# Output projection cut at the last attention head, with its first part placed before that head is finished

## The chip, the cores and the metric

The kernel runs on one core of a Trainium2 chip. The metric is the device time of one execution, in microseconds (us). Before the change it was 695.34 us in three runs (692.23 to 695.98). The span of a trace is a little shorter than the device time: a trace of 688.7 us belongs to a run of 690.84 us.

## The reference

One decoding step of a transformer block: a modulation from a condition vector, attention of one query over a cache of 16,384 positions in 32 heads, output projection, layer norm, and a gated feed-forward block.

```python
h = layernorm(x) * (1 + ca) + sa
q = (h @ wq)                                   # 32 heads of 128
p = softmax(q . k_cache * 128**-0.5)           # 16384 positions per head
o = p . v_cache                                # [32, 128]
x = x + ga * (o.reshape(1, 4096) @ wo)         # output projection, 4096 -> 640
h = layernorm(x) * (1 + cb) + sb
x = x + gb * ((silu(h @ w_gate) * (h @ w_up)) @ w_down)   # 640 -> 1728 -> 640
```

Keys and values are 268 MB of the 290 MB that are read.

## The kernel before

The program keeps a list of instructions for each engine, in the order in which they are added; semaphores order them across engines. `op_P1` sums a key block's products to scores on TensorE, `op_BC` spreads the maximum of the scores over the partitions, `op_EXP` (ScalarE) takes the exponential and the row-sums, `op_PV` multiplies the probabilities with the values ("P.V": 32 matmuls of 512 columns), `op_EV` (ScalarE) copies the result out of PSUM, and `op_OT` turns it into one column per head with four small matmuls.

```python
for h in range(H + 1):
    if h >= 1:
        op_PV(h - 1, 0); op_PV(h - 1, 1)
    if h < H:
        op_P1(h, 0)
    if h >= 1:
        op_OT(h - 1)
    if h < H:
        op_P1(h, 1); op_BC(h)
    # ... V1, V2, V3, NB on VectorE, EV, A3, DG, EXP on ScalarE ...

lsum_ps = pb[0]
pl = prog.add("pe", lambda e: e.matmul(lsum_ps[:, 0:H], lhsT=ones_f, rhs=rowsum[:, 0:H], ...), ...)
d = prog.add("dve", lambda e: e.reciprocal(rinv_all[:, :], lsum_ps[:, 0:H]), ...)
d = prog.add("dve", lambda e: e.tensor_tensor(otn[:, :], otf[:, :], rinv_all[:, :], ALU.mult), ...)

def pe_wo(e):                                   # 160 matmuls of one column
    for j in range(KC):                         # KC = 5 blocks of 128 outputs
        for h in range(H):
            ins = e.matmul(attn_ps[:, j:j + 1], lhsT=wo_v[:, h, j * P:(j + 1) * P],
                           rhs=otn[:, h:h + 1], start=(h == 0), stop=(h == H - 1))
# ... layer norm; 140 gate and up matmuls; silu; 70 down matmuls in four pieces,
#     each waiting for the landing of its piece of the weights; output ...
```

So the projection waits for all 32 heads: the normalisation of the last one stands ahead of all 160 matmuls.

## Time and profile before

| | before |
|---|---|
| span of the trace | 692.0 us |
| transfers: share of the span in which the 16 engines are busy | 98.6%, 420 GB/s |
| last P.V | 661.70 to 670.46 us |
| output projection ends | 677.65 us, 7.19 after the last P.V |
| down projection starts; last down weights land | 687.31; about 685 us |

The page of before shows, in this order, the span, the busy time of each engine with its share and its instructions, the queue of the data transfers (packets, MB, share), and the chain that ended last by engine.

```profile
span 692.0 us, 5506 instructions
...
PE 509.0 (74%) x2434; PEld 210.1 (30%) x2435; DVE 493.0 (71%) x289; ACT 60.8 (9%) x178; POOL 1.5 (0%) x10
...
q1 hardware_dynamic: 18078, 290.48, 98.6%
...
DMA 45%; DVE 28%; PE 23%; ACT 2%; issue 1%; SPq 0%
...
```

The transfers fill the span: 98.6% busy, at 420 GB/s. At that rate the kernel can get much faster only by moving fewer bytes; what remains is how long the tail lasts after the last keys are there. The timeline of before shows that tail. Columns: start in us, duration, engine, line of the kernel, operation, output and inputs, shapes, count; in brackets the idle time of the engine before it and what ended it. "PE" is TensorE's matmuls, "PEld" its weight loads; "issue" is idle time that no recorded dependence explains.

```profile
...
660.30 0.49 PE L533 MATMUL psum_all<-diag,ones_f 128*128 128x128 f32 x2 [1.54 <-ACT diag L527]
...
661.70 8.76 PE L557 MATMUL psum_all<-arena,p_bf 128*4 128x512 bf16 x32 [0.91 <-ACT p_bf L545]
...
670.49 0.59 ACT L565 ACTIVATE ot_sb<-psum_all 4x512 f32<-4x512 f32 x1 [8.84 <-PE psum_all L557]
...
671.13 1.05 PE L574 MATMUL psum_all<-ident_f,ot_sb 4*128 4x1 f32 x8 [0.68 <-ACT ot_sb L565]
...
672.11 0.41 PE L610 MATMUL psum_all<-rowsum,ones_f 128*128 128x32 f32 x2
...
672.55 0.36 DVE L613 RECIPROCAL rinv_all<-psum_all 128x32 f32<-128x32 f32 x1 [11.43 <-PE psum_all L610]
672.94 0.19 DVE L615 TENSOR_TENSOR otn<-otf,rinv_all 128x32 bf16<-128x32 f32 x1
...
673.24 4.41 PE L630 MATMUL psum_all<-otn,arena 128*128 128x1 bf16 x160 [0.72 <-issue]
...
681.45 4.40 PE L672 MATMUL psum_all<-h_bf,arena 128*128 128x1 bf16 x140 [1.14 <-DVE psum_all L663]
...
687.31 2.09 PE L699 MATMUL psum_all<-a_bf,arena 128*128 128x1 bf16 x70 [1.46 <-issue]
...
```

Read it as a chain. The last P.V (L557) ends at 661.70 + 8.76 = 670.46. TensorE then waits 0.68 us for ScalarE's copy (L565), does the transposes (L574) and the row-sum of all heads (L610), and waits 0.72 us, marked "issue", which is really the reciprocal and the multiplication on VectorE (L613, L615). Then come the 160 projection matmuls (L630). The two holes are what the change aims at. TensorE also waits 0.91 us just before the last P.V: a place to put something.

The window view of before, over the last P.V in two parts; the third number from the end is the granted TensorE clock:

```profile
...
661.70:666.00 4.30, 4.30 (x13) 1.39 (x14) 0.00 (x0) 0.00 (x0) 0.00 (x0) 0.60 1.06 377
666.00:670.40 4.40, 4.40 (x21) 1.59 (x19) 0.00 (x0) 0.00 (x0) 0.00 (x0) 1.00 1.03 411
...
```

The first half of the last P.V ran at a mean granted clock of 0.60, the second at 1.00.

### The profile page before, as it was taken

The page shows a single profiled execution, that of the slowest core. Times are in us where ns is not written, and L with a number is a line of the kernel's source. Part 1 is how long each engine was busy: PE and PEld are TensorE (multiplying, and loading weights), DVE is VectorE, ACT ScalarE, POOL GpSimd, SP SyncE. Part 2 cuts the span into 40 slices and gives each one's busy share as a digit, 9 for nine tenths or more (in the row PEclk, how much of TensorE's full clock was granted, in tenths as well). Part 3 has the DMA queues.
Part 4 walks back from the last instruction along what each step waited for, and adds up shares of the span by engine and source line. Part 5 has one row for each costly group of instructions (what it writes and reads, how often), then busy time and mean ns, then how long its engine had stood idle before and what let it go on. Part 6 is the DMA issues. An engine that isn't in the chain of part 4 may idle for free.

```text
span 692.0 us, 5506 instructions
## 1 busy us (share of the span) xinstructions
PE 509.0 (74%) x2434; PEld 210.1 (30%) x2435; DVE 493.0 (71%) x289; ACT 60.8 (9%) x178; POOL 1.5 (0%) x10
## 2 busy tenths in 40 slices
PE   1458868678778768688888685778688677687876
PEld 1222323233332323233333232323223223233335
DVE  1077777778887777778886777778877777778811
ACT  1020100000000000000000000000000000000000
POOL 0000000000000000000000000000000000000000
PEclk9976969878888969688879698877969879888785
DMA  8999999999999999999999999999999999999994
GB/s 345 432 443 425 424 431 444 426 425 428 441 430 427 428 439 429 430 428 435 434 429 428 435 432 430 429 430 435 430 434 427 432 433 434 428 423 437 390 392 158
DMA packets 18101, 290.82 MB, mean 420 GB/s; under 512 B 1244, under 2 KB 7070, under 8 KB 8990
## 3 DMA queue, kind: packets, MB, share of 16 engines
q1 hardware_dynamic: 18078, 290.48, 98.6%
q8 instruction: 19, 0.31, 0.2%
q14 instruction: 4, 0.03, 0.0%
HBM read 290.47 MB, written 0.00 MB: 420 GB/s over the span
## 4 chain that ended last, share of the span: by engine, by line
DMA 45%; DVE 28%; PE 23%; ACT 2%; issue 1%; SPq 0%
DMA arena<-in_A_k_cache_dram 45%; DVE arena L488 16%; PE psum_all L557 14%; DVE arena L494 9%; PE psum_all L506 6%; DVE s_sb L515 1%; PE psum_all L533 1%; ACT diag L527 1%; ACT p_bf L545 1%; PE psum_all L630 1%; PE psum_all L672 1%; DVE m L522 1%; DVE nbias L539 1%; SPq L727 0%; PE psum_all L699 0%
## 5 line engine op out<-in xcount | busy, mean ns | idle before, releaser
L488 DVE TENSOR_TENSOR arena<-arena,qbc 128x8192 bf16<-128x8192 bf16 x64 | 282.9, 4420 | 42.0 <-DMA arena<-in_A_k_cache_dram 41.9
L557 PE MATMUL psum_all<-arena,p_bf 128*4 128x512 bf16 x1024 | 280.5, 443 | 29.1 <-ACT p_bf L545 29.1
L506 PE MATMUL psum_all<-arena,ident_bf 128*128 128x512 bf16 x512 | 151.0, 448 | 72.3 <-DVE arena L494 72.2
L557 PEld LDWEIGHTS psum_all<-arena,p_bf 128*4 128x4 bf16 x1024 | 95.2, 95 | 205.4 <-issue 78.8
L494 DVE TENSOR_TENSOR arena<-arena 128x4096 bf16<-128x4096 bf16 x64 | 146.7, 2292 | 2.2
L506 PEld LDWEIGHTS psum_all<-arena,ident_bf 128*128 128x128 bf16 x512 | 50.8, 109 | 151.8 <-DVE arena L494 79.0
L515 DVE TENSOR_REDUCE s_sb<-psum_all 128x64 f32<-128x512 f32 x64 | 44.0, 687 | 72.4 <-PE psum_all L506 72.4
L533 PE MATMUL psum_all<-diag,ones_f 128*128 128x128 f32 x64 | 19.0, 386 | 49.2 <-ACT diag L527 49.2
L565 ACT ACTIVATE ot_sb<-psum_all 4x512 f32<-4x512 f32 x32 | 18.8, 587 | 283.4 <-PE psum_all L557 283.4
L574 PEld LDWEIGHTS psum_all<-ident_f,ot_sb 4*128 4x128 f32 x256 | 30.8, 186 | 14.3 <-issue 13.1
L539 DVE TENSOR_REDUCE nbias<-psum_all 128x1 f32<-128x128 f32 x32 | 9.3, 291 | 35.8 <-PE psum_all L533 35.8
L574 PE MATMUL psum_all<-ident_f,ot_sb 4*128 4x1 f32 x256 | 33.5, 248 | 0.7 <-ACT ot_sb L565 0.7
L533 PEld LDWEIGHTS psum_all<-diag,ones_f 128*128 128x128 f32 x64 | 11.8, 230 | 71.8 <-ACT diag L527 71.8
L527 ACT ACTIVATE diag<-identS,m 128x128 f32<-128x128 f32 x32 | 12.8, 401 | 188.8 <-DVE m L522 188.8
L456 PE MATMUL psum_all<-arena,h1rep 128*128 128x512 bf16 x39 | 10.9, 449 | 10.0 <-DMA arena<-in_A_wq_dram 10.0
L545 ACT ACTIVATE p_bf<-s_sb,nbias 128x128 bf16<-128x128 f32 x32 | 12.8, 401 | 32.3 <-DVE nbias L539 32.3
L581 ACT ACTIVATE otf<-psum_all 128x1 f32<-128x1 f32 x32 | 5.5, 171 | 73.7 <-PE psum_all L574 73.7
L423 PE MATMUL psum_all<-sc_bf,arena 128*128 128x1 bf16 x150 | 4.1, 165 | 10.1 <-issue 10.1
L429 DVE COPY modT<-psum_all 128x30 f32<-128x30 f32 x1 | 0.2, 191 | 13.7 <-PE psum_all L423 13.7
L522 DVE TENSOR_REDUCE m<-s_sb 128x1 f32<-128x128 f32 x32 | 9.2, 286 | 1.1
L456 PEld LDWEIGHTS psum_all<-arena,h1rep 128*128 128x128 bf16 x40 | 4.5, 113 | 16.0 <-issue 12.9
L613 DVE RECIPROCAL rinv_all<-psum_all 128x32 f32<-128x32 f32 x1 | 0.4, 357 | 11.4 <-PE psum_all L610 11.4
(71 smaller groups left out, 53.4 us busy)
## 6 DMA issues: line engine op xcount, KB each, us to landing
arena<-in_A_k_cache_dram SPq DMA_DIRECT2D x31, 4096.0 KB, 30.9
arena<-in_A_v_cache_dram SPq DMA_DIRECT2D x31, 4096.0 KB, 32.1
arena<-in_A_wo_dram SPq DMA_DIRECT2D x1, 5120.0 KB, 26.5
arena<-in_A_wq_dram SPq DMA_DIRECT2D x1, 4096.0 KB, 24.4
arena<-in_A_k_cache_dram SPq DMA_DIRECT2D x2, 2048.0 KB, 29.3
arena<-in_A_v_cache_dram SPq DMA_DIRECT2D x2, 2048.0 KB, 29.5
arena<-in_w_mod_dram SPq DMA_DIRECT2D x1, 3840.0 KB, 11.8
arena<-in_B_w_gate_dram SPq DMA_DIRECT2D x1, 2160.0 KB, 31.4
```

The costliest lines, as they stand in the source:

```text
L488: v = prog.add("dve", lambda e: e.tensor_tensor(kview, kview, qbc[:, h * DH:(h + 1) * DH].unsqueeze(1).to_broadcast([P, TC, DH]), ALU.mult ...
L494: v = prog.add("dve", lambda e, w_=w_: e.tensor_tensor(kview[:, :, 0:w_], kview[:, :, 0:w_], kview[:, :, w_:2 * w_], ALU.add), waits=[(S_p ...
L506: ins = e.matmul(s4_ps[b][cc][:, 0:TC * CW], lhsT=ident_bf[:, :], rhs=kview[:, :, j * CW:(j + 1) * CW], start=(j == 0), stop=(j == NSTEP - 1))
L515: chk(prog.add("dve", lambda e: e.tensor_reduce(s_sb[b][:, cc * TC:(cc + 1) * TC], s4_ps[b][cc][:, 0:TC * CW].rearrange("p (t c) -> p t c" ...
L522: chk(prog.add("dve", lambda e: e.tensor_reduce(m1[b][:, 0:1], s_sb[b][:, :], AXL.X, ALU.max), waits=[(S_s, vhc(h, NCH - 1))], inc=S_m1), ...
L527: chk(prog.add("act", lambda e: e.activation(diag[b][:, :], identS[:, :], ACTF.Copy, scale=m1[b][:, 0:1]), waits=[(S_m1, v1(h)), (S_pool, ...
L533: chk(prog.add("pe", lambda e: e.matmul(bc_ps[b][:, 0:P], lhsT=ones_f[:, :], rhs=diag[b][:, :], start=True, stop=True), waits=[(S_dg, v1(h ...
L539: chk(prog.add("dve", lambda e: e.tensor_reduce(nbias[b][:, 0:1], bc_ps[b][:, 0:P], AXL.X, ALU.max, negate=True), waits=[(S_bc, v1(h))], i ...
L545: chk(prog.add("act", lambda e: e.activation(p_bf[b][:, :], s_sb[b][:, :], ACTF.Exp, bias=nbias[b][:, 0:1], scale=SCALE, accum_out=rowsum[ ...
L557: ins = e.matmul(ot_ps[b][0:PVG, 0:PVG * DH], lhsT=p_bf[b][:, t0:t0 + PVG], rhs=vview[:, g * PVG:(g + 1) * PVG, :], start=(cc == 0 and g = ...
L565: chk(prog.add("act", lambda e: e.activation(ot4_sb[b][:, :], ot_ps[b][0:PVG, 0:PVG * DH], ACTF.Copy), waits=[(S_pv, vhc(h, NCH - 1))], in ...
L574: ins = e.matmul(bc_ps[b][:, P:P + 1], lhsT=ot4_sb[b][0:PVG, j * DH:(j + 1) * DH], rhs=ident_f[0:PVG, j:j + 1], start=(j == 0), stop=(j == ...
```

## The change

Its intent: TensorE should not wait for the last head. The row-sums of the first 31 heads are normalised before the last P.V, in the hole there. Forty projection matmuls (heads 0 to 7) run while ScalarE copies the last P.V; 115 more (heads 8 to 30) run while VectorE normalises the last head; its five matmuls come last. The five output blocks are now summed side by side, each in a PSUM bank of its own, and three later temporaries move to other banks. Cut to its core:

```diff
+        def early_norm():                      # heads 0..30, ahead of the last P.V
+            pl = prog.add("pe", ... matmul(lsum_ps[:, 0:H - 1], ones_f, rowsum[:, 0:H - 1]) ...)
+            d = prog.add("dve", ... reciprocal(rinv_all[:, 0:H - 1], ...) ...)
+            d = prog.add("dve", ... otn[:, 0:H - 1] = otf[:, 0:H - 1] * rinv_all[:, 0:H - 1] ...)
+        def wo_part(h0, h1, first):
+            for h in range(h0, h1):
+                for j in range(KC):
+                    ins = e.matmul(pb[attn_banks[j]][:, 0:1], lhsT=wo_v[:, h, j * P:(j + 1) * P],
+                                   rhs=otn[:, h:h + 1], start=(h == 0), stop=(h == H - 1))
         for h in range(H + 1):
+            if h == H and SPLIT_WO:
+                early_norm()
             if h >= 1:
                 op_PV(h - 1, 0)
                 op_PV(h - 1, 1)
+            if h == H and SPLIT_WO:
+                wo_part(0, min(8, H - 1), True)
# ... (cut)
-        pl = ... matmul(lsum_ps[:, 0:H], ones_f, rowsum[:, 0:H]) ...
-        pe_v = prog.add("pe", pe_wo, ...)
+            pl = ... matmul(lb_ps[:, 0:1], ones_f, rowsum[:, H - 1:H]) ...   # last head alone
+            d = ... reciprocal and multiply of one column ...
+            wo_part(min(8, H - 1), H - 1, False)
+            wo_part(H - 1, H, False)
# ... (cut: banks of y, o5, tot)
```

## The prediction

> **What bounds the kernel now.** Up to the last head it is the transfers: the page's queue table has the 16 DMA engines busy 98.6% of the span, at 420 GB/s. The change touches nothing there. It touches the tail after the last key block, which the chain of waits shows as one serial chain: last scores, softmax, then the last head's P·V matmuls from 661.70 to 670.47 us, and 21.5 us of dependent small steps to 692.0. The output projection (160 matmuls of one column) is 4.42 us of that.
>
> **The stretch that changes**, from the timeline of before:
> - P·V ends 670.47; PE idles 0.68 us while ScalarE evicts it (0.59 us);
> - transposes of the last head 671.13 to 672.17 (1.05 us);
> - row-sum matmul, ends 672.51;
> - PE idles 0.72 us: reciprocal 0.36, multiply 0.19, and the hand-overs;
> - output projection 673.24 to 677.65.
> So PV-end to projection-end is 7.18 us, of which 1.40 us are PE idle.
>
> **What moves.** The instruction order shows: a row-sum for 31 heads before the last P·V, in a 0.9 us gap (660.80 to 661.70) where PE waits for the exponential; its reciprocal and multiply (about 0.55 us) run on VectorE, idle from 661.1 to 672.5, so free. Forty projection matmuls (8 heads) go between P·V and the transposes; then the transposes, a one-column row-sum, 115 projection matmuls, and 5 for the last head, which alone wait for the last normalisation. Nothing is removed; one two-pass row-sum matmul (about 0.35 us) and two small VectorE operations are added.
>
> **Cost per projection matmul.** In before, 160 take 4.41 us and the 150 of the modulation 4.14 us; less 0.165 us for the last one's own duration, both give 26.7 ns from start to start, at granted clocks 0.50 and 1.00. [...] So I expect the same rate wherever they run. The split uses a bank for each of the five columns[...]. The down projection in before already uses five banks at 30 ns per matmul, so bank switching is cheap.
>
> **New tail, an estimate.** Forty matmuls take 1.07 us, against a 0.68 us hole: the transposes start 0.25 to 0.5 us later, at about 671.5. They end 672.5, the small row-sum about 672.85, 115 matmuls take 3.07 us to about 675.9, the last five 0.3 us: 676.2 instead of 677.65. The last head's normalisation (ready about 673.3) hides. Gain about 1.5 us, all on the chain, 0.2% of the span.
>
> **What could give it back.** The projection's weights land at 667.4 (issued 640.9, 26.5 us): 3 us ahead of the new first use. The last down-projection weights land at about 685; their first use moves from 687.31 to 685.8, still after. Slack shrinks to about 1 us.
>
> **Prediction.** 693.6 us, 80% range 691.0 to 695.9; the spread of before's runs (692.23 to 695.98) is wider than the gain. Chances: faster by 2% 0.01, within 2% 0.98, slower 0.01.
>
> **Signs.** Right: row-sum in the gap before the last P·V; PE without a hole over 0.3 us from P·V to the end of the projection; PV-end to projection-end 5.5 to 6.1 us; everything after unchanged. Wrong: PE waiting for the projection weights right after P·V; more than 30 ns per matmul; a wait for the down weights.
>
> **What would make it wrong.** Late weights; or the PE clock: the last P·V ran at a granted 0.57 from 662 to 666 us, and extra work before it may shift that by up to 2 us either way.

## The result, and the profile after

The changed kernel took 691.43 us, the median of 12 runs (690.48 to 693.71), against 693.5 us for 15 runs of before (690.96 to 695.98). Ratios here are the mean time of one kernel's fast runs over that of the other's fast runs of the same rounds, so they are not quite the ratios of the medians. This one is 0.9969, with a 95% interval of 0.9954 to 0.9984: a gain of 0.31%, about 2.1 us, within 2%, yet clear of noise.

The same lines of the page after the change:

```profile
span 688.7 us, 5514 instructions
...
PE 509.4 (74%) x2436; PEld 210.4 (31%) x2437; DVE 493.3 (72%) x291; ACT 60.7 (9%) x178; POOL 1.5 (0%) x10
...
q1 hardware_dynamic: 18078, 290.48, 99.0%
...
DMA 47%; DVE 26%; PE 19%; SPq 5%; ACT 1%; issue 1%
...
```

The transfers are now busy 99.0% of a shorter span. Some time on the chain has moved to the DMA queue and the landing of the down weights. The timeline of after:

```profile
...
659.61 0.49 PE L533 MATMUL psum_all<-diag,ones_f 128*128 128x128 f32 x2 [1.54 <-ACT diag L527]
...
659.93 0.31 PE L590 MATMUL psum_all<-rowsum,ones_f 128*128 128x31 f32 x2
...
660.34 0.34 DVE L593 RECIPROCAL rinv_all<-psum_all 128x31 f32<-128x31 f32 x1
...
660.72 0.19 DVE L595 TENSOR_TENSOR otn<-otf,rinv_all 128x31 bf16<-128x31 f32 x1
...
661.00 7.07 PE L557 MATMUL psum_all<-arena,p_bf 128*4 128x512 bf16 x32 [0.77 <-ACT p_bf L545]
...
668.00 1.15 PE L608 MATMUL psum_all<-otn,arena 128*128 128x1 bf16 x40
668.11 0.59 ACT L565 ACTIVATE ot_sb<-psum_all 4x512 f32<-4x512 f32 x1 [7.16 <-PE psum_all L557]
...
669.09 1.05 PE L574 MATMUL psum_all<-ident_f,ot_sb 4*128 4x1 f32 x8
...
670.06 0.38 PE L649 MATMUL psum_all<-rowsum,ones_f 128*128 128x1 f32 x2
...
670.31 3.15 PE L608 MATMUL psum_all<-otn,arena 128*128 128x1 bf16 x120
...
677.26 4.57 PE L735 MATMUL psum_all<-h_bf,arena 128*128 128x1 bf16 x140 [1.14 <-DVE psum_all L726]
679.58 2.17 PEld L735 LDWEIGHTS psum_all<-h_bf,arena 128*128 128x128 bf16 x70 [0.17 <-DMA arena<-in_B_w_up_dram]
...
683.33 1.60 PE L762 MATMUL psum_all<-a_bf,arena 128*128 128x1 bf16 x45 [1.50 <-DVE a_bf L751]
683.89 0.96 PEld L762 LDWEIGHTS psum_all<-a_bf,arena 128*128 128x128 bf16 x33 [0.19 <-issue]
685.12 0.83 PEld L762 LDWEIGHTS psum_all<-a_bf,arena 128*128 128x128 bf16 x25 [0.27 <-DMA arena<-in_B_w_down_dram]
685.12 0.91 PE L762 MATMUL psum_all<-a_bf,arena 128*128 128x1 bf16 x25 [0.18 <-DMA arena<-in_B_w_down_dram]
...
```

The early row-sum (L590) stands in the hole before the last P.V. The first 40 projection matmuls start at 668.00, before the last P.V is over at 668.07, and the copy (L565) runs beside them. There is no hole on TensorE up to the end of the projection at 670.31 + 3.15 = 673.46: 5.39 us after the last P.V, where before took 7.19. But the down projection (L762), from 683.33 to 686.03, takes 2.70 us where before took 2.09, with two waits: 0.19 us of weight-load idle marked "issue" after its 12th matmul, and 0.27 us (0.18 on the matmuls) for the down weights.

The window view of after, over the last P.V:

```profile
...
661.00:664.50 3.50, 3.50 (x17) 1.41 (x18) 0.00 (x0) 0.00 (x0) 0.00 (x0) 1.00 1.07 370
664.50:668.00 3.50, 3.50 (x17) 1.23 (x16) 0.00 (x0) 0.00 (x0) 0.00 (x0) 1.00 1.04 398
...
```

So this trace had a luckier clock: 7.07 us for the last P.V against 8.76. The profiled spans differ by 3.3 us, which is not the change's worth. It splits into 0.7 us (the last P.V started at 661.00, not 661.70), 1.69 us (its duration), and 0.9 us for everything after it: 21.5 us from the end of P.V to the end of the span before, 20.6 after. Of the 1.80 us won up to the end of the projection, 0.6 were lost again in the down projection and 0.17 in the gate and up matmuls (4.57 us against 4.40), which waited 0.17 us for the up weights at 679.58. The projection's own weights were nearly late too: issued at 639.35 and 28.2 us under way, they landed about 0.45 us ahead of their first use at 668.00, where the prediction had counted on 3 us.

### The profile page after: what moved, and what is told of

It is laid out like the page before. It is cut to its first block, busy times and chain, and to the rows that moved or that the text cites. A ratio compares the mean times of both kernels' runs of the same rounds, so it can differ in the third digit from the quotient of the medians.

```text
span 688.7 us, 5514 instructions
## 1 busy us (share of the span) xinstructions
PE 509.4 (74%) x2436; PEld 210.4 (31%) x2437; DVE 493.3 (72%) x291; ACT 60.7 (9%) x178; POOL 1.5 (0%) x10
## 4 chain that ended last, share of the span: by engine, by line
DMA 47%; DVE 26%; PE 19%; SPq 5%; ACT 1%; issue 1%
DMA arena<-in_A_k_cache_dram 45%; DVE arena L488 15%; PE psum_all L557 13%; DVE arena L494 8%; PE psum_all L506 5%; SPq L790 5%; DMA arena<-in_B_w_down_dram 2%; DVE s_sb L515 1%; PE psum_all L533 1%; ACT p_bf L545 1%; ACT diag L527 1%; DVE m L522 1%; DVE nbias L539 0%; PE psum_all L574 0%; PE psum_all L762 0%
## 5 line engine op out<-in xcount | busy, mean ns | idle before, releaser
L506 PE MATMUL psum_all<-arena,ident_bf 128*128 128x512 bf16 x512 | 149.1, 444 | 68.0 <-DVE arena L494 68.0
L565 ACT ACTIVATE ot_sb<-psum_all 4x512 f32<-4x512 f32 x32 | 18.8, 586 | 286.6 <-PE psum_all L557 286.6
L464 ACT ACTIVATE qbc<-psum_all 128x512 bf16<-128x512 f32 x8 | 4.8, 597 | 31.9 <-PE psum_all L456 31.9
## 6 DMA issues: line engine op xcount, KB each, us to landing
arena<-in_A_wo_dram SPq DMA_DIRECT2D x1, 5120.0 KB, 28.2
arena<-in_A_wq_dram SPq DMA_DIRECT2D x1, 4096.0 KB, 24.7
```

The costliest lines, as they stand in the source:

```text
L506: ins = e.matmul(s4_ps[b][cc][:, 0:TC * CW], lhsT=ident_bf[:, :], rhs=kview[:, :, j * CW:(j + 1) * CW], start=(j == 0), stop=(j == NSTEP - 1))
L565: chk(prog.add("act", lambda e: e.activation(ot4_sb[b][:, :], ot_ps[b][0:PVG, 0:PVG * DH], ACTF.Copy), waits=[(S_pv, vhc(h, NCH - 1))], in ...
```

## The experiments

Two theories stood at first. H: the filled holes are the gain. C: the early row-sum keeps TensorE busy ahead of the last P.V, and the gain is the better clock there. Later came F: the landing of the last weights sets a floor; and I: instruction fetches interrupt the tail. Each run was timed in five rounds, six runs each, beside before on the same chip: the two down_cut runs and warm_before and warm_after on chip 13, the others on chip 12. So compare the ratios, and not the times, between these two groups. Because the start and the clock of the last P.V change from run to run, the table measures from the end of the last P.V.

| kernel | ratio (95% interval) | last P.V, us | P.V end to projection end | waits on TensorE inside projection, gate/up or down matmuls | P.V end to span end |
|---|---|---|---|---|---|
| before | 1 | 8.76 | 7.19 | none | 21.5 |
| changed | 0.9969 (0.9954 to 0.9984) | 7.07 | 5.39 | 0.17 up landing, 0.19 "issue", 0.27 down landing (weight-load idle) | 20.6 |
| after_again | 0.9973 (0.9952 to 0.9994) | 8.76 | 5.37 | 0.33 | 20.3 |
| early_sum_only | 1.0009 (0.9982 to 1.0037) | 7.07 | 6.78 | 0.40 | 21.8 |
| split_sum_moved | 0.9995 (0.9971 to 1.0020) | 8.75 | 5.38 | none | 19.8 |
| no_eight_first | 0.9989 (0.9965 to 1.0013) | 9.82 | 6.25 | none | 20.7 |
| down_cut_before | 1.0004 (0.9989 to 1.0019) | 7.07 | 7.05 | none | 21.5 |
| down_cut_after | 0.9989 (0.9968 to 1.0009) | 8.76 | 5.38 | none | 19.8 |
| warm_before | 1.0045 (1.0030 to 1.0059) | 7.07 | 8.91 | 1.72 and 1.17 | 24.7 |
| warm_after | 1.0030 (1.0016 to 1.0043) | 7.07 | 6.81 | 0.93 and 1.69 | 23.1 |
| after_shifted | 1.0010 (0.9990 to 1.0029) | 7.07 | 6.34 | 0.79 and 2.79 | 23.8 |
| warm_after_aligned | 0.9971 (0.9953 to 0.9990) | 7.07 | 5.40 | 0.37 | 20.3 |
| warm_before_aligned | 0.9982 (0.9958 to 1.0005) | 7.07 | 7.15 | none | 21.6 |
| warm_aligned_cut | 0.9965 (0.9946 to 0.9984) | 7.07 | 5.38 | none | 19.8 |

### after_again

The changed kernel, no edit.

> The changed kernel once more, unchanged. Theory H (the projection fills the holes of TensorE in the tail): from the end of the last P.V to the end of the projection 5.3 to 5.6 us again (7.18 before), ratio to before 0.997 to 0.998, and the last P.V may be slow (8.8 us) or fast (7.1 us) by chance. Rival C (the gain is the clock: the row-sum in the gap before the last P.V keeps the granted clock up): the last P.V takes 7.1 us again, at a granted clock of 1.00.

It took 690.91 us, ratio 0.9973. The last P.V took 8.76 us, although the early row-sum ran in the hole ahead of it: granted clock 0.59 over 659.8 to 664.0 us, and 1.00 after. The stretch to the end of the projection took 5.37 us as before. So the row-sum does not secure a good clock, and C as stated fails; the 5.4 us repeat. The down projection again waited after its 12th matmul, for 0.33 us, and with no landing named.

### early_sum_only

```diff
# on the kernel before
+            if h == H:
+                early_norm()        # row-sum, reciprocal, multiply of heads 0..30
# ... afterwards the last head's alone; the 160 projection matmuls stay whole
```

> Before plus the early row-sum and normalisation of 31 heads in the gap ahead of the last P.V; the projection stays whole, after the last head's normalisation. Theory H: P.V end to projection end about 6.9 to 7.0 us (only 0.2 us of shorter reciprocal and multiply is won), ratio to before 0.9995 to 1.000. Rival C: the last P.V at 7.1 us, and the ratio 0.9975, most of the change's gain.

The timeline of this kernel:

```profile
...
660.58 7.07 PE L557 MATMUL psum_all<-arena,p_bf 128*4 128x512 bf16 x32 [0.77 <-ACT p_bf L545]
...
670.19 4.24 PE L643 MATMUL psum_all<-otn,arena 128*128 128x1 bf16 x160 [0.50 <-issue]
...
```

The last P.V was fast (7.07 us), by chance or not, and still the kernel gained nothing: ratio 1.0009, where C had asked for 0.9975 (that lies just outside the interval). From P.V end to projection end took 6.78 us, a little under the expected 6.9 to 7.0: the hole ahead of the projection (0.50 us "issue") is 0.22 us shorter, with reciprocal and multiplication of one column, and the 160 matmuls took 0.17 us less (4.24 against 4.41). The early normalisation alone is not the gain.

### split_sum_moved

```diff
# on the changed kernel: only the row-sum matmul moves; its VectorE part stays
+            if h == H - 1 and SPLIT_WO:
+                early_sum()
             if h < H:
                 op_P1(h, 1)
```

> The changed kernel with its early row-sum moved ahead of the second half of the last scores, so that the gap before the last P.V is bare as in before; the projection is still split. Theory H: P.V end to projection end 5.3 to 5.6 us, ratio to before 0.997 to 0.998. Rival C: the last P.V back at 8.8 us and the ratio at 0.999 to 1.000.

The timeline of this kernel:

```profile
...
656.10 0.41 PE L590 MATMUL psum_all<-rowsum,ones_f 128*128 128x31 f32 x2
...
661.72 8.75 PE L557 MATMUL psum_all<-arena,p_bf 128*4 128x512 bf16 x32 [0.91 <-ACT p_bf L545]
...
672.71 3.14 PE L611 MATMUL psum_all<-otn,arena 128*128 128x1 bf16 x120
...
685.57 2.12 PE L767 MATMUL psum_all<-a_bf,arena 128*128 128x1 bf16 x70 [1.50 <-DVE a_bf L756]
...
```

The times cannot decide: the ratio 0.9995 is what C expected, and so is the slow last P.V (8.75 us), but the interval holds H's 0.998 too. The trace decides for the stretch: 5.38 us without any row-sum in the hole. It is also the clean case of the change: P.V ended late (670.47), the down projection took 2.12 us without a wait, and P.V end to span end is 19.8 us, 1.7 less than before. Three of the six runs lay at 693.7 to 694.0; they have no trace here, but a slow last P.V (8.75 us, against 7.07 in after) costs 1.68 us, about as much as the change wins. Whether the row-sum in the hole makes a good clock more frequent remains open: among the traces without warming dummies, the last P.V behind it took 7.07 us in three (after, early_sum_only, after_shifted) and 8.76 to 9.82 in three (after_again, down_cut_after, no_eight_first); without it, 7.07 in one and 8.75 to 8.76 in two.

### no_eight_first

```diff
-                wo_part(0, min(8, H - 1), True)
+                wo_part(0, 0, True)
-            wo_part(min(8, H - 1), H - 1, False)
+            wo_part(0, H - 1, True)
```

> The changed kernel without the 40 projection matmuls between the last P.V and the transposes: all 155 follow the small row-sum. Theory H: the hole of 0.68 us is back, P.V end to projection end 6.0 to 6.2 us; of these 0.7 us part may hide behind the landing of the down weights, so ratio to before 0.9975 to 0.999. Rival C: no change against the changed kernel.

The timeline of this kernel:

```profile
...
662.09 9.82 PE L557 MATMUL psum_all<-arena,p_bf 128*4 128x512 bf16 x32 [0.64 <-ACT p_bf L545]
...
673.80 4.36 PE L608 MATMUL psum_all<-otn,arena 128*128 128x1 bf16 x160
...
```

The hole of 0.68 us for the copy is back, and P.V end to projection end is 6.25 us: 0.86 to 0.88 more than with the 40 matmuls in front, a little over the expected 6.0 to 6.2. That is the hole, and 0.2 us of slower matmuls: 160 took 4.36 us, 26.4 ns from start to start, against 25.1 in after. The last P.V took 9.82 us here, at a clock of 0.50 up to 667 us, again with the row-sum ahead of it. The ratio, 0.9989, lies where H put it, but its interval holds 1 as well as the changed kernel's 0.9969.

### down_cut_before and down_cut_after

```diff
# only the first of the four pieces of the down weights is loaded; all 70 matmuls run, on stale data
+            if i == 0:
+                late_items.append(itw)
+                wd_first = itw
+            wd_pieces.append((f0, f1, wd_first))
```

Their outputs are wrong, which doesn't matter for the times.

> Before with only the first of four pieces of the down weights loaded (wrong result on purpose; the same matmuls read stale data, 1.36 MB fewer bytes to load). Theory F (the tail is a race of the compute chain against the landing of the last weights, about 685 us, and before is mostly late in that race): ratio to before 0.999 to 1.000, no wait ahead of the down projection, which takes 2.1 us. Rival D (transfers set the time of both kernels): 1 to 3 us faster, ratio 0.996 to 0.998.

> The changed kernel with only the first piece of the down weights loaded (wrong result on purpose). Theory F: the landing floor is gone, so the down projection takes 2.1 us without a wait (2.7 before), the fastest runs fall below the 690.46 us that no run of the changed kernel has beaten, to about 689.5; ratio to before 0.9955 to 0.997. Against the cut kernel before, the whole 1.8 us of the filled holes show. Rival: no floor, ratio as for the changed kernel, 0.997 to 0.998, and the fastest runs at 690.4.

Cutting 1.36 MB from the kernel before gained nothing (ratio 1.0004), as F said: it is late in the race against the landing, and D fails. The changed kernel with the cut gave 0.9989, with an interval of 0.9968 to 1.0009: F's 0.9955 to 0.997 was missed. Against the cut kernel before it led by 1.06 us in the mean, and not by F's 1.8. Its fastest runs, 689.80 and 689.95, do lie below the 690.46 us of all 18 runs of the changed kernel, as F asked; but they ran on another chip than after_again, one on which before's fastest run was lower as well (690.63 against 691.46). And the profiled run had a slow P.V (8.76 us), so it says nothing of the floor. Inconclusive; the clock had to be held still.

### warm_before and warm_after

```diff
# dummy matmuls of 128 columns into a bank not in use, in TensorE's waits of the last two heads
                 op_P1(h, 1)
+                if h >= H - 2:
+                    warm(10, P)
                 op_BC(h)
+                if h == H - 2:
+                    warm(9, P)
# and ahead of the last P.V: warm(5, P) in the changed kernel, warm(8, P) in before
```

> Before with dummy matmuls (into a bank not in use) in the waits of TensorE around the last two heads' scores, so that its clock is not lowered before the last P.V; nothing else. If the spread of both kernels' runs is the chance of a lowered clock in that stretch: last P.V 7.1 us, median 691.3 to 692.0, and no run over 693; ratio to before 0.997 to 0.999. If not: the last P.V slow at times, and spread and median as before.

> The changed kernel with the same dummy matmuls. With the fast P.V each time, the compute chain comes ahead of the landing of the down weights: theory F says that all runs then sit on the floor, median 690.6 to 690.9, spread under 1 us, ratio to before 0.9955 to 0.997, and only 1 us or less against the warm kernel before (not the 1.8 us of the filled holes). Without a floor: 689.7, 1.8 us under the warm kernel before.

The last P.V was fast in both, and yet both kernels were slower than before on the same chip (692.18 us): 695.21 and 694.12 us, by 3.0 and 1.9. Every expected median, ratio and spread was missed; only the difference between the two, 0.93 us in the mean, was within the expected 1 us. The traces showed why: two waits marked "issue" in the middle of unbroken runs of matmuls, in before after 155 of 160 projection matmuls (1.72 us) and in both after 118 of 140 gate and up matmuls (1.17 and 1.69 us). Nothing that a semaphore orders stands there. Counted back, the two places are about 256 TensorE instructions apart. The trace of before has 19 packets of 16,384 bytes on the instruction queue (q8), and its page 4869 matmuls and weight loads of TensorE: by these, an estimate, about 256 to a packet. That made theory I.

### after_shifted

```diff
# on the changed kernel, right after the modulation matmuls, in a 10 us wait for the query weights
+            for _ in range(34):
+                ins = e.matmul(bc_ps[0][:, 0:1], lhsT=ident_bf[:, :], rhs=ident_bf[:, 0:1], start=True, stop=True)
```

> The changed kernel with 34 dummy matmuls of one column early, in the wait for the query weights (TensorE is idle there for 10 us), and nothing in the tail: they only shift all later instructions of TensorE by 68. Theory I (the waits in the middle of the projection and of the gate matmuls in the warm kernels are fetches of the next 16 KB block of 256 instructions, late because the transfers fill the engines, and the added instructions moved the block boundaries there): waits of about 1 to 1.7 us each after some 115 of the 120 later projection matmuls and after gate matmul 118, median 692.5 to 693.5, ratio to before 1.000 to 1.003. Rival J (the dummy matmuls next to the last heads do the harm themselves): as the changed kernel, no such wait, ratio 0.997.

TensorE's timeline of this kernel:

```profile
...
670.99 3.04 PE L615 MATMUL psum_all<-otn,arena 128*128 128x1 bf16 x116
674.82 0.27 PE L615 MATMUL psum_all<-otn,arena 128*128 128x1 bf16 x4 [0.79 <-issue]
675.74 0.58 PE L710 MATMUL psum_all<-s,ones_f 128*128 128x1 f32 x2 [0.65 <-DVE s L708]
677.17 0.59 PE L720 MATMUL psum_all<-s,ones_f 128*128 128x1 f32 x2 [0.85 <-ACT sqj L718]
678.89 3.60 PE L742 MATMUL psum_all<-h_bf,arena 128*128 128x1 bf16 x118 [1.14 <-DVE psum_all L733]
685.27 0.95 PE L742 MATMUL psum_all<-h_bf,arena 128*128 128x1 bf16 x22 [2.79 <-issue]
...
```

Thirty-four harmless matmuls 650 us earlier, and the tail has two waits of 0.79 and 2.79 us, at the same instructions as in warm_after. Between the two waits lie 4 + 118 matmuls with their weight loads (244 instructions) and two sums of two passes each (8): 252 recorded instructions, and a few that are not recorded. The kernel took 694.6 us (ratio 1.0010), against 691.43 and 690.91 unshifted: it lost the whole gain, and more in the median than was expected (692.5 to 693.5); the waits were expected at 1 to 1.7 us each. J fails: the harm is in the position, not in the dummies near the last heads.

### warm_after_aligned, warm_before_aligned, warm_aligned_cut

```diff
# warm_after plus 94 early dummies, warm_before plus 91: in both 128 matmuls, 256 instructions of shift
# warm_aligned_cut: warm_after_aligned plus the cut of the down weights
```

> The changed kernel with the warming dummies, and 94 dummies early, so that the shift is 256 instructions in all and every later boundary stands where the changed kernel has it. Theory I: the two long waits are gone, last P.V 7.1 us, median 690.5 to 691.0, spread under 1 us, ratio 0.996 to 0.9975. Rival J: 693 to 694 again.

> Before with the warming dummies and 91 early ones, 256 instructions of shift in all. Theory I: no long waits, last P.V 7.1 us, median 691.5 to 692.0, ratio 0.998 to 0.999; so the changed kernel's gain over it is about 1 us or less, since with a fast P.V the landing of the weights and one block fetch take up part of the 1.8 us. Rival J: 695 again.

> The warm aligned changed kernel with only the first piece of the down weights loaded (wrong result on purpose): the test of the landing floor that the chance of the clock had blurred. Theory F: down projection 2.1 to 2.4 us with no wait for a landing, 0.3 to 0.7 us faster than the warm aligned changed kernel, median 689.9 to 690.5. Rival (no floor): the same median within 0.2 us.

The timeline of warm_after_aligned:

```profile
...
656.00 2.85 PE L513 MATMUL psum_all<-arena,ident_bf 128*128 128x512 bf16 x8 [2.90 <-DVE arena L501]
...
661.79 7.07 PE L564 MATMUL psum_all<-arena,p_bf 128*4 128x512 bf16 x32 [0.49 <-ACT p_bf L552]
...
678.05 4.40 PE L756 MATMUL psum_all<-h_bf,arena 128*128 128x1 bf16 x140 [1.14 <-DVE psum_all L747]
...
683.96 0.46 PE L783 MATMUL psum_all<-a_bf,arena 128*128 128x1 bf16 x12 [1.50 <-DVE a_bf L772]
...
684.78 1.80 PE L783 MATMUL psum_all<-a_bf,arena 128*128 128x1 bf16 x58 [0.37 <-issue]
...
```

With a shift of 256 the long waits are gone: ratio 0.9971 (691.71 us) instead of 1.0030, and 0.9982 (692.54 us) instead of 1.0045. Theory I holds: the waits stand at a fixed count of instructions, and a whole block's shift puts them back. What is left stands where the changed kernel had it, after the 12th down matmul (0.37 us).

The traces also record the packets of the instruction queue (q8 in `--dma`), and these tie the waits to fetches. Each packet has 16,384 bytes; 19 of them are in a trace, and 20 in the three with a shift of 256. After each of the ten waits of the table that no landing ended, TensorE went on 2.3 to 2.6 us after such a packet had begun (in after_shifted 672.51 and 682.66 us, and TensorE went on at 674.82 and 685.27).

With both kernels warm, the changed one leads by 0.75 us in the mean (691.70 against 692.45), within the "1 us or less" that was expected, though their intervals overlap. The traces give 21.6 and 20.3 us from the end of P.V.

The timeline of warm_aligned_cut has the down projection as one group:

```profile
...
684.41 2.10 PE L784 MATMUL psum_all<-a_bf,arena 128*128 128x1 bf16 x70 [1.50 <-DVE a_bf L773]
...
```

It takes 2.10 us without a wait, and P.V end to span end is again 19.8 us, against 20.3 with all weights. The times agree with F: 691.20 against 691.71 us, 0.5 less, though single runs overlap. Its gate matmuls began 0.45 us later than those of warm_after_aligned (678.50 against 678.05 us), which alone might hide a wait of 0.37 us; but the fetch's packet came 2.44 us earlier (679.74 against 682.18), and the last data ended at 680.95 instead of 684.60. So the give-back is real and tied to the transfers at the end. In this pair it shows as a late fetch and not as a late landing; in the profile of the changed kernel it showed as both.

The dummies did not make the run times as even, nor the medians as low, as expected. In four of the five warm traces the P.V of the head before was fast as well (7.07 us), so that TensorE then waited for VectorE (2.90 us above), and the last scores (L513 above) took 2.64 to 3.59 us, against 1.90 in before and in after. In before, eight such matmuls took 3.59 us at a granted clock of 0.50 (637.23 us) and 1.90 at 1.00 (656.86 us); by these, an estimate, the slow stretch moved from the P.V to the scores. No version tried beats the changed kernel: its 691.57 us in the mean (690.91 in the median of the later runs) is not undercut by a kernel with a right result, though the 691.70 of warm_after_aligned is too near to call.

## Why the prediction was right

The measured 691.43 us lies in the range of 691.0 to 695.9, and the forecast gain (1.7 us from the 695.34 of the first three runs) compares with 2.1 us measured. That the time fell into the range says little, and is in part luck: the range is more than twice as wide as the gain, before's own median of 693.5 lies in it, and 691.43 is only 0.43 from its edge. What counts is the mechanism. Point by point:

- **The holes.** "PV-end to projection-end 5.5 to 6.1 us" was measured as 5.37 to 5.39 in three traces of the split. The gain was 1.8 us and not 1.5: the two holes of 0.68 and 0.72, about 0.26 from faster matmuls (next point), and the remaining 0.14 from overlaps, since the 40 matmuls start 0.07 us before the last P.V ends and the 120 start while the small row-sum still runs. The transposes began 1.02 us after P.V, as estimated (671.5 less 670.47).
- **The cost of a matmul.** 26.7 ns from start to start was estimated, "wherever they run". In after, 120 took 3.15 us, which less 0.165 for the last is 25.1 ns; over 160 matmuls the difference is 0.26 us. The granted clock was 1.00 there up to 673.2 us, and 0.50 in the projection of before. Banks are not the cause: in early_sum_only all 160 go to one bank, and matmul by matmul its trace has 25.1 ns while the clock is at 1.00 and 26.7 ns after it has fallen to 0.50. The estimate took the rate to be the same at both clocks because the modulation's 150 showed 26.7 ns at 1.00. That 1.00 is no measurement: no trace here has a record of the clock before 32 us (the first in before is at 34.5), and the view prints 1.00 where there is none. What the clock was there is not shown. The mean in the projection at a clock of 1.00 was 25.0 to 25.4 ns in the 13 traces that have such a stretch.
- **"Row-sum in the gap before the last P.V", normalisation free on VectorE.** Right.
- **"Everything after unchanged", "slack shrinks to about 1 us".** This step failed. The slack had been counted on one trace with a slow P.V, and instruction fetches had no place in it. Where P.V ends near 668 us, as in the profile of after, the up weights (679.5 us), the last down weights (about 685 us) and a block fetch are late, and 0.5 to 0.9 us of the gain goes back. Late landing had been named as a sign of being wrong, but only the landing; the fetch was not foreseen.
- **The absolute time.** 693.6 was high because its base was: three runs gave 695.34, fifteen 693.5.
- **The clock.** "May shift that by up to 2 us either way" was right in size (7.07, 8.76 or 9.82 us for the same P.V). P.V's slow part lasted 3.41 us in before (662.54 to 665.95, at 0.50) and was absent in after. What sets its place and its length is not shown.

What stays open: the measured gain (1.1 to 3.2 us) is centred above the 0.9 to 1.7 us that the traces show after the last P.V. Chance is enough for that, and a better chance of a good clock would be too. That a fetch is late because data fill the transfer engines rests on the packets of one pair, warm_after_aligned and warm_aligned_cut. Why TensorE goes on only some 2.5 us after a packet begins is not shown; the longest wait of after_shifted ended at 685.27 us, 2.6 us after its packet had begun, while the data queue was busy for 49, 19 and 9% of the three us from 682 and not at all from 685.

## What to carry to other kernels

When the tail of a kernel is one chain, put work that does not need the last result into its holes, and check each hole by its own duration: here they were 0.68 and 0.72 us, and both were won. Measure such a gain from an event near it (the end of the last P.V), because the start of the tail moves by more than the gain from run to run (the last P.V ended at 668.07 us in after and at 671.91 in no_eight_first, whose programs are the same up to there). And long runs of tiny matmuls pass through instruction blocks quickly: in before the 160 of the projection and their weight loads, 320 instructions, took 4.41 us. An edit far ahead can shift the block boundaries in the tail, as 34 early matmuls did here (ratio 1.0010 against 0.9969), so a small slowdown after adding harmless instructions may be only that; pad to a whole block before blaming the edit (here a shift of 256 instructions brought 1.0030 back to 0.9971).
